# A memory-transformer block beside a mixer MLP: half of a weight loaded after the mixer's output stage, a fifth transpose buffer, segment sums and two constants later, one value product later in the tail

## The chip, the core and the metric

The kernel runs on one core of a Trainium2 chip. The metric is the device time in microseconds: the median of five runs, 1518.0 us before the change (1517.87 to 1518.15). A core has a matrix engine (TensorE, PE in the profile, with its weight loads shown apart as PEld), VectorE (DVE), ScalarE (ACT), GpSimd (POOL) and SyncE (SP, which here only issues DMA transfers). Each engine runs its own list of instructions in order; semaphores make one wait for another. Matmul results go to PSUM, a small memory from which DVE or ACT must take them before the buffer can be used again.

## What is computed

```python
xn = _layernorm(x)
return x + _A_ref(xn, ...) + _B_ref(xn, ...)

def _B_ref(x, w1, w2, w3, w4):                  # 2048 tokens, D = 1024, F = 3584
    h = _gelu(_layernorm(x) @ w1)
    ...                                         # four channel groups shifted by -1, +1, -2, +2 tokens
    x1 = x + hs                                 # hs = shifted h @ w2
    return x1 + _gelu(_layernorm(x1) @ w3) @ w4

def _A_ref(x, mem0, Wq, Wk, Wv, Wo, seg_len):   # 32 heads of 128, 8 memory rows, segments of 32 tokens
    for s in range(n_seg):
        h = concatenate([mem, xs])
        q, k, v = h @ Wq, h @ Wk, h @ Wv
        o = softmax(mask(q k^T * scale)) v @ Wo
        mem, out = o[:M], o[M:]
```

## The kernel before, in words

The program is written out by hand in the order in which each engine runs it. There are four stages, one after the other on PE.

**Start and w1 (lines 170 to 322).** x comes in 16 tiles of 128 tokens. For each tile DVE takes statistics (`ln_stats`, lines 199 to 207, the last step a power on POOL), writes a normalised copy (`ln_apply`, line 218; POOL makes the bias `nm` at line 220), and the copy is transposed. The first four tiles are transposed by PE (`pe_trans`, line 243, cast out of PSUM by DVE at 246 and ACT at 248), the others by a DMA transpose from SP's queue (`dma_trans`, line 223), behind which the next x tile and later w2 and w3 are queued. ACT overwrites x with its normalised form (`normalise_x`, line 235). Two tiles make a group; group g is multiplied by w1 in eight chains of eight matmuls (line 258 for groups 1 to 7, line 283 for group 0), and ACT takes each chain out of PSUM with a GELU (260, 288). The chains rotate through four PSUM buffers, "mm". Group 0 uses two larger buffers, "A" and "B", which the segment sums use after it: `seg_sums(n)` multiplies x tile n by the constant `segone`, 128x4, in eight small matmuls (line 253), and ACT copies the result to `xs` (254). Constants are loaded from POOL's queue by `const_tile` (line 106).

**Mixer output, w2 (lines 327 to 357).** For each of 16 tiles, two chains of eight matmuls (336); DVE adds x and takes statistics, POOL finishes them, ACT writes the normalised `xn3` (348, a ring of four buffers), POOL's queue stores x1 to a scratch tensor (349), and SP's queue transposes xn3 into `xn3T` (350). Behind each of the first eight transposes SP has one load of w3 (448 KB, `load_w3`, line 155). w3 has two halves of eight such pieces: w3a (0 to 7), w3b (8 to 15).

**MLP, w3 and w4 (lines 359 to 538).** SP's queue first loads the last four pieces of w3b, then w4 in seven loads of 1 MB, then what the residual needs (R and xt, 436 to 438). For each of four blocks of 512 tokens, PE runs 28 chains over w3 (514; chains 0 to 13 read w3a, 14 to 27 w3b), with a GELU by ACT (515), then w4 (532). `eye9` is used once at the start of this stage (372). Chunks of Wv and Wo are loaded in between (382, 384) into the place of an xn3T that PE has finished with.

**Attention (lines 545 to 913).** 32 steps (4 token blocks by 8 groups of 4 heads). In each step, PE projects q, k and v (579, 595, 602), and between these chains runs the score matmuls of the previous step's four sub-blocks (`scores`, 624, PSUM buffer "A") and the value products (`values`, 654, PSUM buffer "B"). DVE adds a term while it takes the product to `oX` (658), then ACT copies the memory columns to `oTm` (662), and the buffer is free. The output projection sums 32 heads (`out_part`, 751). After the last step s there is a hand-written tail (lines 880 to 912), in which scores and values of s alternate with output parts of 28 heads; p is the step before s. Its first lines are

```python
            scores(s, 0)
            values(p, 3)
            out_part(b, 0, 0, hp)
            scores(s, 1)
            values(s, 0)
            out_part(b, 1, 0, hp)
```

Of the kernel before, what the change touches and what calls it, by code (L numbers as in the profile page):

```python
# [13 lines left out]
BF16 = mybir.dt.bfloat16  # L14
# [7 lines left out]
P = 128  # L22
S = 2048
D = 1024
# [7 lines left out]
M = 8  # L32
# [31 lines left out]
def kernel(  # L64
# [37 lines left out]
    def const_tile(name, arr, dt=BF16, later=False):  # L102
        a = _bf(arr) if dt == BF16 else np.asarray(arr, np.float32)
        d = nc.inline_tensor(a, name=name)
        t = cpool.tile(list(arr.shape), dt, name=name + "_sb")
        load = lambda: nc.gpsimd.dma_start(t[:], d.ap())
        if later:
            return load, t
        load()
        return t  # L110

    tok = np.arange(P)
    segone_np = (tok[:, None] // SEG == np.arange(4)[None, :]).astype(np.float32)
# [5 lines left out]
    neghalf = cpool.tile([P, 2], F32)  # L119
    nc.gpsimd.memset(neghalf[:], -0.5)  # L120
    ident = const_tile("c_ident", np.eye(P, dtype=np.float32))
    segone = const_tile("c_segone", segone_np)
    eye9 = const_tile("c_eye9", np.concatenate([np.eye(M, dtype=np.float32), np.ones((M, 1), np.float32)], 1))
    load_qones, qones = const_tile("c_qones", np.repeat(segone_np[:, :, None], P, axis=2), later=True)
    load_causal, causal = const_tile("c_causal", causal_np, F32, later=True)
    load_mask40, mask40 = const_tile("c_mask40", _mask40(False), later=True)
# [36 lines left out]
    with ExitStack() as keepx:  # L163
# [6 lines left out]
        with ExitStack() as p0:  # L170
# [102 lines left out]
            pe_trans(1)  # L273
            normalise_x(0)
            normalise_x(1)
            first = []
            for tag in "AB":
                t = aux_tile([P, 2, 512], tag, "ps1")
# [14 lines left out]
            ln_stats(3)  # L293
            for n in (2, 3):
                ln_apply(n)
            for c0 in range(0, KT, 2):
                w1_first(c0, range(4, KT))
                w1_first(c0 + 1, range(4, KT))
                w1_first_out((c0, c0 + 1))
                if c0 in (2, 4):  # L300
                    pe_trans(c0 // 2 + 1)
            seg_sums(0)
            seg_sums(1)
            ln_stats(4)
            for g in range(1, NT // 2):
                nxt = [n for n in (2 * g + 2, 2 * g + 3) if n < NT]
                for n in nxt:
                    if n + 1 < NT:
                        ln_stats(n + 1)
                    ln_apply(n)  # L310
                    dma_trans(n)
                stage1(g, range(4))
                if g == 1:
                    normalise_x(2)
                    normalise_x(3)
                for n in nxt:
                    normalise_x(n)
                stage1(g, range(4, KT))
                seg_sums(2 * g)
                seg_sums(2 * g + 1)  # L320
# [6 lines left out]
        with ExitStack() as p2:  # L327
            ring = p2.enter_context(tc.tile_pool(name="p2ring", bufs=4))
            for n in range(NT):
                x1 = ring.tile([P, D], F32, tag="x1")  # L330
                st = ring.tile([P, 2, 6], F32, tag="st")
                for ch in range(2):
                    ps = mm_tile("ps2")
                    for k in range(KT):
                        o = 2 + n * P + SH[k]
                        nc.tensor.matmul(ps[:], hTB[:, k, o:o + P], w2_sb[:, k, ch * 512:(ch + 1) * 512], start=(k == 0), stop=(k == KT - 1))  # L336
                    nc.vector.tensor_tensor(x1[:, ch * 512:(ch + 1) * 512], ps[:], xts[n][:, ch * 512:(ch + 1) * 512], op=ALU.add)
                    nc.vector.bn_stats(st[:, ch, :], x1[:, ch * 512:(ch + 1) * 512])
                mv = ring.tile([P, 2], F32, tag="mv")
                nc.vector.bn_aggr(mv[:], st[:])  # L340
                a = ring.tile([P, 1], F32, tag="a")
                nc.gpsimd.tensor_scalar(a[:], mv[:, 1:2], EPS, None, op0=ALU.add)
                r3 = ring.tile([P, 1], F32, tag="r3")
                nc.gpsimd.tensor_tensor(r3[:], a[:], neghalf[:, 0:1], op=ALU.pow)
                nm3 = ring.tile([P, 1], F32, tag="nm3")
                nc.gpsimd.tensor_scalar(nm3[:], mv[:, 0:1], r3[:], -1.0, op0=ALU.mult, op1=ALU.mult)
                xn3 = ring.tile([P, D], BF16, tag="xn3")
                nc.scalar.activation(xn3[:], x1[:], ACTF.Identity, bias=nm3[:], scale=r3[:])
                nc.gpsimd.dma_start(R1_v[:, n, :], x1[:])
                nc.sync.dma_start_transpose(xn3Ts[n // 4][:, n % 4, :, :], xn3[:])  # L350
                if n < 8:
                    load_w3(4 + n)
                elif n == 8:
                    load_qones()
                    load_causal()
                    load_mask40()

    attx = main.enter_context(ExitStack())
    with ExitStack() as p3:
        big = p3.enter_context(tc.tile_pool(name="p3big", bufs=1))  # L360
        ring = p3.enter_context(tc.tile_pool(name="p3ring", bufs=3))
        for i in range(12, 16):
            load_w3(i)
        w4t = []
        for c in range(7):
# [448 lines left out]
    for i in range(NS):  # L814
        s = new_step(i)
        p = steps.get(i - 1)
        pp = steps.get(i - 2)
        fz = p is not None and p.b == 0
        last = i == NS - 1
        hooks = {}  # L820

        def at(c, f, *a):
            hooks.setdefault(c, []).append((f, a))

        if pp is not None:
            at(1, values, pp, 3)
        if p is not None:
            at(0, scores, p, 0)
            for m in range(3):
                at(3 * m + 3, scores, p, m + 1)  # L830
                at(3 * m + 4, values, p, m)
        if 4 < s.hg and s.b + 1 < NB:
            for k in range(3 * s.hg - 15, min(3 * s.hg - 12, KT)):
                at(2 + 4 * (k % 3), make_xm, s.b + 1, (k,))
        if fz:
            at(4, first_scores, p)
            at(8, first_soft, p)
            at(11, first_trans, p)
        if pp is not None and pp.b == 0:
            at(1, first_values, pp)  # L840
        if s.hg == 1 and s.b > 0:
            for c in range(8):
                at(1, out_chain, s.b - 1, c)
        if s.hg == 2 and s.b > 0:
            at(2, norm_sums, s.b - 1)
            for j in range(4):
                at((4, 5, 7, 8)[j], norm_recip, s.b - 1, j)
            at(10, norm_apply, s.b - 1)
            at(11, norm_add, s.b - 1)
        if s.hg == 0 and s.b > 0:  # L850
            load_Rt(s.b - 1, 0)
            load_Rt(s.b - 1, 1)
        for c in range(12):
            if c < 4:
                if c == 0 and s.b == 0:
                    mem_proj(s, "q", QM)
                q_chain(s, c)
                if c == 0:
                    mem_cols(s)
                if c == 3:  # L860
                    if i + 1 < NS:
                        need_w("k", i + 1)
                    if s.b == 0:
                        nc.sync.dma_start(wo_sb[:, hsl(s.hg), :], Wo_v[:, hsl(s.hg), :])
                    if s.hg == 4 and s.b + 1 < NB:
                        load_xT(s.b + 1)
            elif c < 8:
                k_chain(s, c - 4)
                if c == 7 and i + 1 < NS:
                    need_w("v", i + 1)  # L870
            else:
                v_chain(s, c - 8)
                if c == 11:
                    if s.b == 0:
                        mem_proj(s, "v", VM)
                    if i + 2 < NS:
                        need_w("q", i + 2)
            for f, a in hooks.get(c, ()):
                f(*a)
        if last:  # L880
            b = s.b
            load_Rt(b, 0)
            load_Rt(b, 1)
            hp = H - 4
            scores(s, 0)
            values(p, 3)
            out_part(b, 0, 0, hp)
            scores(s, 1)
            values(s, 0)
            out_part(b, 1, 0, hp)  # L890
            scores(s, 2)
            values(s, 1)
            out_part(b, 0, hp, H)
            out_part(b, 1, hp, H)
            out_part(b, 2, 0, hp)
            scores(s, 3)
            values(s, 2)
            out_part(b, 3, 0, hp)
            values(s, 3)
            out_part(b, 2, hp, H)  # L900
            out_part(b, 3, hp, H)
            norm_sums(b)
            for j in range(4):
                norm_recip(b, j)
            norm_apply(b)
            norm_add(b)
            out_chain(b, 4)
            out_chain(b, 5)
            verify()
            out_chain(b, 6)  # L910
            verdict()
            out_part(b, 7, 0, H, 2)
# [129 lines left out]
```

## Time and profile before

| | |
|---|---|
| median of 5 runs | 1518.0 us |
| the profiled execution | 1518.11 us |
| its span, first to last instruction | 1516.2 us |
| granted TensorE clock | 1.000 |
| busy: PE, DVE, ACT, POOL | 1497.0, 661.3, 453.1, 235.6 us |
| bytes moved by DMA | 208.38 MB, mean 137 GB/s |

A row of the order in time has the start and the duration in us, the engine, the line of the kernel, the operation, its output and inputs with their shape, how many instructions are merged in the row, and, in brackets, how long the engine was idle before it and what ended that. In PE's rows an instruction's end is modelled, so rows can overlap a little; starts are the better measure. SPq rows are DMA issues: they show when SP issued a transfer and for how long it was held up, not the transfer itself. A row that merges instructions can have gaps inside. The list of waits has who waited for whom, the total us, how many times, and the longest.

### The profile page before, as it was taken

What the parts mean: (1) busy time and instruction counts of PE and PEld (TensorE: products, weight loads), DVE (VectorE), ACT (ScalarE), POOL (GpSimd) and SP (SyncE); (2) the same over time, 40 slices, a digit from 0 to 9 for tenths busy, and PEclk for the clock granted to TensorE, in tenths of its full rate; (3) what the DMA queues carried; (4) which work ended last, traced back from release to release, by engine and by line L of the source; (5) the groups of instructions that cost most, each with busy time, mean ns of one, the idle gap of its engine ahead of it and who ended that gap; (6) DMA issues with size and microseconds to landing.
All of it is one profiled execution on the core that took longest, in us unless ns stands there. A gap on an engine that the chain in (4) does not pass through costs nothing.

```text
span 1516.2 us, 23927 instructions
## 1 busy us (share of the span) xinstructions
PE 1497.0 (99%) x9456; PEld 793.4 (52%) x9582; DVE 661.3 (44%) x1555; ACT 453.1 (30%) x1249; POOL 235.6 (16%) x652
## 2 busy tenths in 40 slices
PE   8999999999999999999999999999999999999998
PEld 6844444444444466666544444444544444444446
DVE  7284010010110226666622856731767640675652
ACT  5633202103012035454401344310433420344320
POOL 3142110111110211221200111110111110111100
PEclk9999999999999999999999999999999999999999
DMA  6699553553122545574522454421464431444211
GB/s 184 173 251 310 193 188 98 175 174 138 63 91 50 186 152 168 159 204 142 179 70 83 140 166 139 154 87 60 138 170 144 140 111 53 125 142 141 84 34 39
DMA packets 191029, 208.38 MB, mean 137 GB/s; under 512 B 51192, under 2 KB 158856, under 8 KB 190912
## 3 DMA queue, kind: packets, MB, share of 16 engines
q1 hardware_dynamic: 183664, 182.49, 39.9%
q0 software_dynamic: 7248, 24.31, 4.2%
q8 instruction: 77, 1.26, 0.3%
q14 instruction: 40, 0.33, 0.1%
HBM read 170.07 MB, written 25.17 MB: 129 GB/s over the span
## 4 chain that ended last, share of the span: by engine, by line
PE 97%; DVE 1%; ACT 1%; issue 1%; DMA 0%; DVEq 0%; ACTq 0%
PE psK L595 15%; PE psQ L579 15%; PE psP L751 15%; PE psV L602 14%; PE ps L514 13%; PE ps L532 13%; PE ps L336 4%; PE ps L258 3%; PE psO L654 2%; PE psS L624 2%; PE psM L611 1%; PE psY L773 1%; PE psvb L396 1%; PE psG L405 1%; PE ps L283 0%
## 5 line engine op out<-in xcount | busy, mean ns | idle before, releaser
L751 PE MATMUL psP<-wo_sb,oX 128*128 128x512 bf16 (+1 forms) x1036 | 221.5, 372 | 1.1
L628 ACT ACTIVATE ET<-psS 32x132 f32<-32x132 f32 x512 | 139.0, 272 | 195.3 <-PE psS L624 189.7
L532 PE MATMUL ps<-w,hT_all 128*128 128x512 bf16 x874 | 193.7, 379 | 1.2
L595 PE MATMUL psK<-xT,w 128*128 128x512 bf16 x747 | 176.3, 379 | 1.1
L579 PE MATMUL psQ<-xT,w 128*128 128x512 bf16 x750 | 175.9, 379 | 1.1
L602 PE MATMUL psV<-w,xT 128*128 128x512 bf16 x745 | 175.0, 379 | 1.0
L751 PEld LDWEIGHTS <-oX 128*128 128x128 bf16 x1056 | 102.8, 98 | 115.5
L595 PEld LDWEIGHTS <-w 128*128 128x128 bf16 x1280 | 121.3, 98 | 80.2
L579 PEld LDWEIGHTS <-w 128*128 128x128 bf16 x1024 | 96.8, 98 | 105.5 <-issue 1.3
L515 ACT ACTIVATE hT_all<-ps 128x512 bf16<-128x512 f32 x112 | 66.7, 597 | 283.9 <-PE ps L514 283.9
L532 PEld LDWEIGHTS <-hT_all 128*128 128x128 bf16 x896 | 87.2, 98 | 103.8
L662 ACT CAST oTm<-psO 128x16 bf16<-128x16 f32 x128 | 23.0, 179 | 357.1 <-DVE oX L658 357.1
L630 DVE STREAM_TRANSPOSE EQ<-ET 128x128 f32<-128x128 f32 x128 | 39.8, 311 | 172.3 <-ACT ET L628 172.0
L586 DVE TENSOR_TENSOR Q<-psQ,QM 128x512 bf16<-128x512 f32 (+1 forms) x128 | 85.3, 679 | 61.2 <-ACT Q L585 43.2
L645 POOL TENSOR_TENSOR BD<-ET,c_segone_sb 128x16 bf16<-128x16 f32 x128 | 33.9, 265 | 494.2 <-ACT ET L628 494.2
L602 PEld LDWEIGHTS <-xT 128*128 128x128 bf16 x768 | 72.1, 98 | 73.5
L514 PE MATMUL ps<-xn3T,w3a 128*128 128x512 bf16 x448 | 97.7, 379 | 0.0
L514 PE MATMUL ps<-xn3T,w3b 128*128 128x512 bf16 x448 | 97.7, 379 | 0.0
L643 DVE TENSOR_TENSOR BD<-PT,c_segone_sb 128x512 bf16<-128x512 bf16 x128 | 90.0, 703 | 4.4
L757 DVE TENSOR_TENSOR ot<-psP,Rt 128x512 bf16<-128x512 f32 (+1 forms) x33 | 22.2, 675 | 155.8 <-PE psP L751 155.8
L596 ACT CAST K<-psK 128x512 bf16<-128x512 f32 (+1 forms) x160 | 78.8, 506 | 33.6 <-PE psK L595 33.0
L440 DVE TENSOR_SCALAR xt<-xt,lnst 128x1024 bf16<-128x1024 bf16 x16 | 8.7, 546 | 181.7 <-POOL R L439 181.7
(157 smaller groups left out, 1619.4 us busy)
## 6 DMA issues: line engine op xcount, KB each, us to landing
w<-in_A_Wq_dram SPq DMA_DIRECT2D x32, 1024.0 KB, 5.7
w<-in_A_Wk_dram SPq DMA_DIRECT2D x32, 1024.0 KB, 5.7
w<-in_A_Wv_dram SPq DMA_DIRECT2D x32, 1024.0 KB, 5.7
R_scratch<-x POOLq DMA_DIRECT2D x16, 512.0 KB, 6.7
R<-R_scratch SPq DMA_DIRECT2D x16, 512.0 KB, 7.7
chunk<-in_A_Wv_dram SPq DMA_DIRECT2D x8, 1024.0 KB, 6.1
R_scratch<-R POOLq DMA_DIRECT2D x16, 512.0 KB, 6.4
chunk<-in_A_Wo_dram SPq DMA_DIRECT2D x8, 1024.0 KB, 6.4
```

The lines of the kernel that those rows point to most:

```text
L336: nc.tensor.matmul(ps[:], hTB[:, k, o:o + P], w2_sb[:, k, ch * 512:(ch + 1) * 512], start=(k == 0), stop=(k == KT - 1))
L514: nc.tensor.matmul(ps[:], w3[:, k, (f % FH) * P:(f % FH + 1) * P], xn3Ts[tb][:, :, k, :], start=(k == 0), stop=(k == KT - 1))
L515: nc.scalar.activation(h3T[:, f, :], ps[:], ACTF.Gelu_apprx_tanh)
L532: nc.tensor.matmul(ps[:], h3T[:, f, j * P:(j + 1) * P], w4t[f // 4][:, f % 4, ch * 512:(ch + 1) * 512], start=(f == 0), stop=(f == FT - 1))
L579: nc.tensor.matmul(ps[:], w[:, k, hh * P:(hh + 1) * P], s.xm[:, k, 0:512], start=(k == 0), stop=(k == KT - 1))
L586: nc.vector.tensor_tensor(q3[:, j0:16, 0:SEG], p3_[:, j0:16, :], QM[:, 4 * s.hg + hh, z + j0:z + 16].unsqueeze(2).to_broadcast((P, 16 - j0 ...
L595: nc.tensor.matmul(ps[:, 0:c], w[:, k, hh * P:(hh + 1) * P], s.xm[:, k, h2 * c:(h2 + 1) * c], start=(k == 0), stop=(k == KT - 1))
L596: nc.scalar.copy(s.K[:, hh, h2 * c:(h2 + 1) * c], ps[:, 0:c])
L602: nc.tensor.matmul(ps[:], s.xm[:, k, m * P:(m + 1) * P], w[:, k, :], start=(k == 0), stop=(k == KT - 1))
L628: nc.scalar.activation(ET[q, :, :], ps[q, :, W * j:W * (j + 1)], ACTF.Exp, scale=SCALE)
L643: nc.vector.tensor_tensor(B4[:, :, :, 0:SEG], PT[:].unsqueeze(2).to_broadcast((P, 4, 4, SEG)), so.unsqueeze(3).to_broadcast((P, 4, 4, SEG) ...
L751: nc.tensor.matmul(ps[:, 0:w], oX[:, h, m * P:(m + 1) * P], wo_sb[:, h, cc], start=(h == 0), stop=(h == H - 1))
```

## The change

Five edits. `segone` and `eye9` are no longer loaded at the top but on POOL's queue behind the first two tiles' normalisation. `ln_stats(4)` moves ahead of the second half of group 0, and the segment sums of tiles 0 and 1 from the end of group 0 to the middle of group 1, ahead of `normalise_x(2)` and `(3)`. The ring of `xn3` gets a fifth buffer. Only the first four transposes of the mixer's output stage are followed by a w3 load; all eight pieces of w3b are loaded at the start of the MLP stage, ahead of w4. In the tail, `values(p, 3)` comes after the first output part instead of before it. No matmul is added or removed.

```diff
-    segone = const_tile("c_segone", segone_np)
-    eye9 = const_tile("c_eye9", np.concatenate([np.eye(M, dtype=np.float32), np.ones((M, 1), np.float32)], 1))
+    load_segone, segone = const_tile("c_segone", segone_np, later=True)
+    load_eye9, eye9 = const_tile("c_eye9", np.concatenate([np.eye(M, dtype=np.float32), np.ones((M, 1), np.float32)], 1), later=True)
...
             normalise_x(0)
             normalise_x(1)
+            load_segone()
+            load_eye9()
...
             for n in (2, 3):
                 ln_apply(n)
+            ln_stats(4)
             for c0 in range(0, KT, 2):
...
                 if c0 in (2, 4):
                     pe_trans(c0 // 2 + 1)
-            seg_sums(0)
-            seg_sums(1)
-            ln_stats(4)
...
                 stage1(g, range(4))
                 if g == 1:
+                    seg_sums(0)
+                    seg_sums(1)
                     normalise_x(2)
                     normalise_x(3)
...
-                xn3 = ring.tile([P, D], BF16, tag="xn3")
+                xn3 = ring.tile([P, D], BF16, tag="xn3", bufs=5)
...
-                if n < 8:
+                if n < 4:
                     load_w3(4 + n)
...
-        for i in range(12, 16):
+        for i in range(8, 16):
             load_w3(i)
...
             scores(s, 0)
+            out_part(b, 0, 0, hp)
             values(p, 3)
-            out_part(b, 0, 0, hp)
             scores(s, 1)
```

## The prediction

> **What bounds the kernel now.** I read the page's head and its first two parts, then the chain of waits, then TensorE's own waits, and last the order in time at the three places that the change touches.
>
> ```profile
> span 1516.2 us, 23927 instructions
> ...
> PE 1497.0 (99%) x9456; PEld 793.4 (52%) x9582; DVE 661.3 (44%) x1555; ACT 453.1 (30%) x1249; POOL 235.6 (16%) x652
> ...
> PEclk9999999999999999999999999999999999999999
> ...
> PE 97%; DVE 1%; ACT 1%; issue 1%; DMA 0%; DVEq 0%; ACTq 0%
> ```
>
> TensorE (PE) is busy for 1497.0 of 1516.2 us, at full granted clock, and is 97% of the chain that ended last. The change adds and removes no matmul. So it can only give back part of the 1516.2 - 1497.0 = 19.2 us in which PE is idle, or add to them. PE's waits say where those lie:
>
> ```profile
> PE ps L258 <- ACT hT_all L260: 1.4, 1, 1.4
> ...
> PE psO L654 <- ACT oTm L662: 1.0, 1, 1.0
> PE psX L253 <- ACT hT_all L288: 0.6, 1, 0.6
> ```
>
> The columns are total us, times, longest. These three, 3.0 us in all, stand where the change works. The rest is elsewhere: the table by stretches has 4.6 us of idle in the first 20 us and 3.8 in the last 16, and about 0.05 per 10.8 us between. PE's order in time around the first two waits:
>
> ```profile
> 20.09 0.34 PE L253 MATMUL psX<-c_segone_sb,x 128*128 128x4 bf16 x8
> 20.99 0.34 PE L253 MATMUL psX<-c_segone_sb,x 128*128 128x4 bf16 x8 [0.57 <-ACT hT_all L288]
> 21.20 7.15 PE L258 MATMUL ps<-xn2T,w_sb 128*128 128x256 bf16 x64
> 28.18 0.54 PE L253 MATMUL psX<-c_segone_sb,x 128*128 128x4 bf16 x16
> 30.11 7.15 PE L258 MATMUL ps<-xn2T,w_sb 128*128 128x256 bf16 x64 [1.39 <-ACT hT_all L260]
> ```
>
> ScalarE (ACT) in the same stretch:
>
> ```profile
> 24.89 0.38 ACT L260 ACTIVATE hT_all<-ps 128x256 bf16<-128x256 f32 x1 [0.49 <-PE ps L258]
> 25.17 4.62 ACT L235 ACTIVATE x<-x,nm,lnst 128x1024 bf16<-128x1024 bf16 x4
> 29.69 1.18 ACT L260 ACTIVATE hT_all<-ps 128x256 bf16<-128x256 f32 x4
> ```
>
> The four normalisations hold ACT for 4.5 us, PE fills its four PSUM buffers meanwhile, and waits until the first GELU after them.
>
> **Segment sums, one group later.** Before, the sums of tile 1 wait for ACT to empty the accumulator that they reuse, so group 1 starts at 21.20. Now w1's group 1 comes straight after the last first-group matmuls. Its PSUM buffers must be emptied by the transposes' casts, and ln_stats(4) now stands before those on VectorE (DVE): the stats take 21.21 - 19.34 = 1.87 us and would run 16.12 to 17.99, so tile 2's cast moves from 17.41 to 17.99. Tile 3's cast still waits for PE at 18.73 and ends at 19.42. Both are done before 20.1: no cost, with 0.7 us of cover; without it, what is late is PE itself. x of tile 4 is there: DMA engines fall idle near 15 us and its statistics show no DMA wait. Group 1 then starts at about 20.1, 1.1 us earlier.
>
> That isn't kept in full. Four chains later (GELU 3 was at 21.20 + 3.69) GELU 3 ends at about 24.2 instead of 25.27. Now the 16 small matmuls follow (0.40 us of PE) and ACT has two xs copies (0.28 for the pair in the later row) ahead of the normalisations. The second copy needs its sums, at 20.11 + 3.53 + 0.54 = 24.18, and ends at about 24.4. So the normalisations start at about 24.35 instead of 25.17, and PE's restart at 30.11 moves by the same 0.8 us, to 29.3. PE itself arrives at 28.0 (28.72 before) and still waits about 1.3 us: the wait stays nearly whole, ACT's chain decides. **Gain 0.8 us.** From below: 0.3, if copies and normalisations don't overlap. From above: 1.1, the whole shift of the group's start. The inputs of group 2 come sooner too: DVE's chain for tiles 4 and 5 loses the 1.87 us that the stats stood behind, so the transpose of tile 5 goes to SyncE's queue (SP) at 24.1 instead of 25.98. With the landing times of this tile, 3.2 to 5.2 us, it is there by 29.3 at the worst.
>
> **Two constants later on GpSimd (POOL).** Their issues, 0.557 and 0.538 us, leave 1.99 to 3.07, where POOL next waits 2.56 us for DVE: nothing is gained there. They go behind the nm pair that ends at 9.02, and end at about 10.1; POOL's next operation is at 12.75. The data, 7.2 us from issue to landing, are there by 16.8; segone is first read at 23.6, eye9 at 129.8. One doubt: DVE's normalisation of tile 1 starts at 9.07 for 0.54 us, and PE's transposes wait for it. Rows first: the POOL power op takes 0.70 us alone (12.75) and 0.92 beside such a DVE op (14.61), while thirteen of these DVE ops keep to 535 to 545 ns whatever POOL does. The Trainium skill, "SBUF — State Buffer", section "Who interferes with whom", states that a DVE op in a two-port mode and a GpSimd op exclude each other for a whole instruction, and that the first to issue wins. By the rows POOL loses and PE pays nothing. By the rule, POOL would issue 0.05 us earlier, win, and cost PE up to 0.56 us in the start-up. No run here shows a POOL DMA issue beside this DVE op; I take the rows, 0, and keep 0.56 for the range.
>
> **Half of w3 behind the mixer's output stage, and a fifth xn3 buffer.** In that stage PE is busy 4.95 to 5.00 of every 5 us, so quicker transposes (ACT waited 3.8 us once for a buffer) give PE nothing: 0. What moves are four loads of 448 KB on SP, to the end of the transposes. SP's order there:
>
> ```profile
> 137.16 2.19 SPq L155 DMA_DIRECT2D w3b<-in_B_w_dram  x4
> 139.85 12.37 SPq L367 DMA_DIRECT2D w<-in_B_w_dram  x7
> 152.27 2.58 SPq L436 DMA_DIRECT2D R<-R_scratch  x1
> 154.90 0.56 SPq L438 DMA_DIRECT2D xt<-in_A_x_dram  x1
> 178.61 0.38 SPq L382 DMA_DIRECT2D chunk<-in_A_Wv_dram  x1
> ```
>
> PE first reads w3b at 154.24, now at 153.4. The last xn3 is ready at 134.47 - 0.8, and the transposes have less ahead of them, so the eight loads begin at about 136. Eight loads are 3.67 MB; at the 370 to 390 GB/s that the table shows from 140 on, 10 us plus landing put the last at 147 to 148: 5 us of cover. Behind them stand w4 (first read at 178.4; the DMA engines fell idle at 165, now by about 169), the first R and xt (0.5 and 0.25 MB, consumed by POOL at 167, now 171; DVE adds into R only after 184), and then SP waits 23.1 us for PE before the next load. All of the 4.75 us (1.84 MB at 387 GB/s) is swallowed by that. **Cost 0.** If the cover fails, PE stalls at f = 14 for whatever is missing.
>
> **Tail.** PE now, with the wait:
>
> ```profile
> 1444.21 0.39 PE L624 MATMUL psS<-Q,K 128*128 128x132 bf16 x4
> 1445.64 0.41 PE L654 MATMUL psO<-BD,V 128*128 128x132 bf16 x4 [1.04 <-ACT oTm L662]
> 1445.89 6.20 PE L751 MATMUL psP<-wo_sb,oX 128*128 128x512 bf16 x28
> 1451.93 0.39 PE L624 MATMUL psS<-Q,K 128*128 128x132 bf16 x4
> 1452.16 0.40 PE L654 MATMUL psO<-BD,V 128*128 128x132 bf16 x4
> ```
>
> values(p, 3) waits for the one psO buffer. After the change the 28 heads start at 1444.21 + 0.24 = 1444.45 (their buffer was emptied at about 1441; they read token block 0 of oX, values(p, 3) writes block 3), and values(p, 3) follows 6.04 us later, at 1450.49, without a wait. But values(s, 0) wants the same psO only two steps later. How long a psO is held, an undisturbed case tells: matmuls at 1473.17, DVE's oX 1473.61 to 1474.30, ACT's oTm 1474.34 to 1474.52, and 0.06 to PE: 1.41 us. So values(s, 0) can start at 1451.90, not at 1450.96: a new wait of about 0.95 us takes the place of the one removed. Against 1452.16 before, **gain 0.26 us**. Bounds: 0, if the new wait is as long as the old (1.2 by start times), and 1.2, if it is hidden. Behind the waiting matmuls stands the whole of out_part 1; scores(s, 1) has its exponentials after oTm on ACT, which 6 us of out_part cover.
>
> **Sum.** 0.8 + 0 + 0 + 0.26 = 1.06 us. The profiled execution took 1518.11 us (span 1516.2 and 1.9 around it), 0.11 above the median; a span of 1515.1 gives 1517.05 in its terms, and against the median of 1518.0, 1516.95. I say 1517.0. A measurement can tell about 0.2%, 3.0 us: by size this is no change.
>
> **Rivals.**
> - The waits only move (chance 0.20): ACT gives back only 0.3 us at group 2, the tail's new wait equals the old, and POOL's issues cost part of 0.56: 1518.0 - 0.3 + 0.2 = 1517.9. For it speaks that both places have a second wait just behind the first; against it, the computed starts.
> - More than I count (0.10): the whole 1.1 at group 1 and a hidden psO, 1518.0 - 2.1 = 1515.9. It needs ACT's chain not to bind, against the row at 25.17.
> - w3b comes late (0.08), the slower side. Between 136 and 153.4 the queue must bring 3.67 MB, beside about 1 MB of R1 writes still going out: 4.7 MB in 17.4 us is 270 GB/s, and below that PE stalls at f = 14. Between 120 and 140 the table shows 184, 274, 353 and 268 GB/s, with transposes among the loads, so it isn't out of reach. At 200 GB/s it takes 23.5 us, 6.1 too late: 1517.0 + 6.1 = 1523.1. Against it: the loads come after the transposes, and from 140 on the rate was never below 370 while loads were queued.
> - My forecast, 0.6. The last 0.02 are left for faster by over 3 us: there isn't that much idle time at these places, so only an effect that I don't see could give it.
>
> Faster by over 0.2% 0.02, within 0.2% 0.90, slower by over 0.2% 0.08. The range 1515.8 to 1518.2 takes in the first two rivals and leaves out the third.
>
> **What would show it.** Group 1's first w1 matmul near 20.1 and group 2's near 29.3, with a wait of about 1.3 us for ACT there; DVE's second normalisation still at 9.07; no PE wait at the first w3b matmul near 153.4; in the tail no wait at the first psO and one of about 0.8 us, in that list's way of counting, at the next. I am wrong if PE waits for a DMA anywhere between 130 and 190, or if a PE wait shows elsewhere that was not there before.

## The result and the profile after

The changed kernel takes 1516.76 us (median of 42 runs, 1516.42 to 1517.67), the kernel before 1518.16 (79 runs beside them, 1517.54 to 1532.09). The ratio of the means is 0.9979, with a 95% interval of 0.9970 to 0.9987: faster by 0.21%, not the 0.07% that I forecast. The medians alone differ by 1.40 us, close to my 1.06. The rest is in the spread, which the five times that I had did not show: of the 79 runs of the kernel before, 22 took more than 1519 us; of the 42 after, none. Without those 22, the median before is 1518.08. So there are two effects: 1.32 us in the typical execution, and about 1.9 us in the mean (1520.03 - 1516.80 - 1.32) from executions that are now and then 1 to 14 us longer and that the change took away. Below I call a run long when it is over 1519 us.

The profiled execution after took 1516.79 us. The page's head, PE's waits and PE's order in time around the first two waits:

```profile
span 1514.9 us, 23923 instructions
...
PE 1497.5 (99%) x9456; PEld 793.5 (52%) x9582; DVE 661.5 (44%) x1555; ACT 452.4 (30%) x1249; POOL 235.3 (16%) x652
```

```profile
PE ps L258 <- ACT hT_all L260: 1.2, 1, 1.2
...
PE psO L656 <- ACT oTm L664: 0.8, 1, 0.8
```

```profile
20.05 3.66 PE L258 MATMUL ps<-xn2T,w_sb 128*128 128x256 bf16 x32
23.54 0.54 PE L253 MATMUL psX<-c_segone_sb,x 128*128 128x4 bf16 x16
23.95 3.65 PE L258 MATMUL ps<-xn2T,w_sb 128*128 128x256 bf16 x32
27.44 0.54 PE L253 MATMUL psX<-c_segone_sb,x 128*128 128x4 bf16 x16
29.17 7.15 PE L258 MATMUL ps<-xn2T,w_sb 128*128 128x256 bf16 x64 [1.19 <-ACT hT_all L260]
```

Group 1 starts at 20.05 instead of 21.20, group 2 at 29.17 instead of 30.11: 0.94 us, of which 0.04 came before the edits' place. ACT's normalisations start at 24.21 (24.35 expected). In the tail:

```profile
1443.22 0.39 PE L626 MATMUL psS<-Q,K 128*128 128x132 bf16 x4
1443.45 6.21 PE L753 MATMUL psP<-wo_sb,oX 128*128 128x512 bf16 x28
1449.50 0.40 PE L656 MATMUL psO<-BD,V 128*128 128x132 bf16 x4
1449.73 0.39 PE L626 MATMUL psS<-Q,K 128*128 128x132 bf16 x4
1450.89 0.41 PE L656 MATMUL psO<-BD,V 128*128 128x132 bf16 x4 [0.76 <-ACT oTm L664]
```

From the first scores to the second values product it is now 7.67 us, where it was 1452.16 - 1444.21 = 7.95: a gain of 0.28, with the new wait where it was expected. PE reads w3b from 153.30 on without a wait. All of this is as forecast, and none of it explains the 22 long executions of the kernel before.

What the two profiles do show on that is in the mixer's output stage. In these two, a transpose of xn3 took 3.1 to 12.8 us to land before (median 5.8), and 3.1 to 6.8 after (median 4.4). In the table by stretches, the last two columns are the busy share of the DMA engines and the GB/s that they moved. The share adds up the time that packets took, so overlapping packets bring it above 1. Before, then after:

```profile
120.00:125.00 5.00, 5.00 (x25) 2.29 (x24) 4.10 (x8) 1.25 (x2) 1.83 (x5) 1.00 1.15 184
125.00:130.00 5.00, 4.95 (x30) 2.21 (x29) 4.31 (x8) 1.98 (x3) 2.87 (x8) 1.00 1.20 274
```

```profile
120.00:125.00 5.00, 5.00 (x25) 2.25 (x23) 4.34 (x8) 1.24 (x1) 2.59 (x7) 1.00 0.87 244
125.00:130.00 5.00, 4.95 (x31) 2.25 (x30) 4.25 (x8) 2.48 (x2) 2.34 (x6) 1.00 0.74 203
```

In the profile before, the DMA engines are saturated until the stage ends; in the one after, they have caught up. ACT's last normalisation of the stage and its first GELU of the MLP, before:

```profile
124.18 1.24 ACT L348 ACTIVATE xn<-x,nm,r 128x1024 bf16<-128x1024 f32 x1 [3.75 <-DMA xn3T<-xn]
...
133.23 1.24 ACT L348 ACTIVATE xn<-x,nm,r 128x1024 bf16<-128x1024 f32 x1 [2.31 <-POOL nm L346]
134.38 1.66 ACT L515 ACTIVATE hT_all<-ps 128x512 bf16<-128x512 f32 x3
```

PE starts the MLP at 130.06, and its four PSUM buffers hold four chains of 1.73 us, until 136.97. The first GELU empties one at 134.98: 2.0 us of cover. The GELU stands on ACT behind the last xn3, and an xn3 can't be written before an old transpose has left its buffer. That gave my theory, A: when the transposes land a few us later than in this profile, ACT stands still, and PE with it. The rivals were B, that the edits of group 1 or of the tail took the long executions away, and C, chance or the chip.

### The profile page after: what moved, and what is told of

The parts are those of the page before. It is cut to its first block, busy times and chain, and to the rows that moved or that the text cites. A ratio compares the mean times of both kernels' runs of the same rounds, so it can differ in the third digit from the quotient of the medians.

```text
span 1514.9 us, 23923 instructions
## 1 busy us (share of the span) xinstructions
PE 1497.5 (99%) x9456; PEld 793.5 (52%) x9582; DVE 661.5 (44%) x1555; ACT 452.4 (30%) x1249; POOL 235.3 (16%) x652
## 4 chain that ended last, share of the span: by engine, by line
PE 95%; DVE 2%; ACT 1%; issue 1%; DMA 0%; DVEq 0%; ACTq 0%
PE psP L753 15%; PE psQ L581 14%; PE psK L597 14%; PE psV L604 14%; PE ps L516 13%; PE ps L534 13%; PE ps L338 4%; PE ps L258 3%; PE psO L656 2%; PE psS L626 2%; PE psM L613 1%; PE psY L775 1%; PE psvb L398 1%; PE psG L407 1%; PE ps L285 0%
```

## The experiments

### Which edit takes the long executions away

All four ran on one chip beside 67 runs of the kernel before, of which 19 were long.

Mixer stage undone in the changed kernel:

```diff
-                xn3 = ring.tile([P, D], BF16, tag="xn3", bufs=5)
+                xn3 = ring.tile([P, D], BF16, tag="xn3")
...
-                if n < 4:
+                if n < 8:
...
-        for i in range(8, 16):
+        for i in range(12, 16):
```

> The changed kernel with the mixer's output stage as before (four xn3 buffers, eight w3 loads behind its transposes). The typical execution: 1516.8 us, like the changed kernel, since that stage's edits gave PE nothing in the two profiles. Theory A (that stage's transfers now and then hold up PE, and the change took that away): about a quarter of the executions come out 2 to 14 us longer again, as 20 of 79 did before. Rival B (the group 1 or tail edits took it away): no execution over 1518. Rival C (chance, or the chip): long executions on some chips with every kernel.

Measured: 3 of 14 long, median 1516.95; without the long ones 1516.86. The long executions are back. The other one of the pair is the reverse, the kernel before with these three lines changed and nothing else:

> The kernel before with only the mixer stage's edits (fifth buffer, half of w3 later). Typical execution 1518.0 us by both theories. Theory A: no long executions, none over 1519. Rival B: about a quarter are 2 to 14 us longer, as before.

Measured: none of 22 long, 1517.70 to 1518.38, median 1517.89, ratio 0.9988 (0.9977 to 0.9999). B falls: this stage's edits alone do it, and with them the typical execution changes little (1517.89 against 1518.02, the median of the kernel before without its long runs). C is unlikely: all ran on one chip, and with 19 of 67 long, a kernel that is no different would show none in 22 about once in 1500 times. Then each half of the edit, the first with only the second and third of the hunks above:

> The changed kernel with all eight w3 loads back behind the mixer's transposes, the fifth xn3 buffer kept. Typical 1516.8 us. Theory A in the form that the loads' traffic delays transposes and x1 stores: long executions come back (a tenth to a quarter). In the form that the missing fifth buffer is the cause: none. Rival B: none.

Measured: 5 of 22 long (up to 1534.46), median 1516.88. And with only the first hunk:

> The changed kernel with four xn3 buffers instead of five, the w3 loads late. Typical 1516.8 us. Theory A in the form that the loads' traffic is the cause: no long executions. In the form that the fifth buffer is what helps: a tenth to a quarter long. Rival B: none.

Measured: 1 of 22 long (1529.02), median 1516.78. Where the loads stand is what counts: with them back, 5 of 22 are long, as before; with them late, one, and that few would come by chance in under 1% of cases if the kernel were like the one before. One in 22 is too few to say whether the fifth buffer takes away a rest.

### Where the time goes in a long execution

The changed kernel, with four buffers and all of w3 in the stage:

```diff
-                xn3 = ring.tile([P, D], BF16, tag="xn3", bufs=5)
+                xn3 = ring.tile([P, D], BF16, tag="xn3")
...
-                if n < 4:
+                if n < 12:
                     load_w3(4 + n)
-                elif n == 8:
+                if n == 8:
...
-        for i in range(8, 16):
-            load_w3(i)
```

> The changed kernel with four xn3 buffers and all twelve remaining w3 pieces behind the mixer stage's first twelve transposes, none after: four more loads in that stage than before. Theory A (the loads' traffic delays that stage's transposes and stores until PE runs out of PSUM buffers): at least as many long executions as the 3 of 14 and 5 of 22 with eight loads, likely a third or more, and longer ones; in the profile transposes that take over 10 us to land, waits of ACT for xn3T and of DVE for the x1 stores, of several us. Typical execution 1516.8 to 1519. Rival (what counts is only where w3b's first pieces stand, not the traffic): no more long ones than with eight loads.

Measured: 11 of 14 long, beside 16 of 51 for the kernel before, median 1526.87, up to 1540.08, and the profiled execution is a long one (1529.86). Its waits, and ACT's and PE's order in time where the stage ends:

```profile
ACT xn L350 <- DMA xn3T<-xn: 22.6, 4, 8.0
...
PE ps L514 <- ACT hT_all L515: 11.4, 1, 11.4
```

```profile
136.50 1.24 ACT L350 ACTIVATE xn<-x,nm,r 128x1024 bf16<-128x1024 f32 x1 [5.37 <-DMA xn3T<-xn]
145.73 1.24 ACT L350 ACTIVATE xn<-x,nm,r 128x1024 bf16<-128x1024 f32 x1 [7.99 <-DMA xn3T<-xn]
146.88 2.04 ACT L515 ACTIVATE hT_all<-ps 128x512 bf16<-128x512 f32 x4
```

```profile
129.02 7.08 PE L514 MATMUL ps<-xn3T,w3a 128*128 128x512 bf16 x32
147.51 18.79 PE L514 MATMUL ps<-xn3T,w3a 128*128 128x512 bf16 x80 [11.41 <-ACT hT_all L515]
```

PE runs through the mixer stage without a break, makes four chains of the MLP (32 matmuls), and then waits 11.4 us. The GELUs are next on ACT, but the normalisations of the last tiles stand ahead of them, the very last waiting 8 us for a transpose. No one needs these tiles before the MLP's last block.

The kernel before once more, and the two other edits by themselves:

> The kernel before once more, for its profile. By the counts so far (41 of 146 over 1519 us) one such look is long with a chance of about 0.28; Theory A expects then a PE wait in the mixer stage or at its end, behind late transposes or stores. Otherwise 1518.0 us and a profile like the first.

It was not a long one: 1518.2 us, transposes landing after at most 9.0 us. The second profile of it went the same way, 1518.2 us and at most 10.7:

> The kernel before, for a profile of a long execution (about one in three of its executions on these chips). Theory A: if long, the PE stall lies at the MLP's fifth chain, for ACT behind late transposes. If short, a profile like the first.

So a long execution of the kernel before itself was never profiled; that its stall is at the same place is inferred from its variants. Its recorded clocks fit that. Of the 195 runs of the kernel before beside these experiments, the 38 with a mean granted clock of 0.998 or less are all long, by over 4 us. The three long executions that were profiled (this one with twelve loads and two below) had 0.997, 0.997 and 0.994, and there it is PE's standstill that lowers the clock. Where PE stands still the mean can't tell.

> The kernel before with only the edits of the first stage: constants later, statistics and segment sums moved. My sum for it was 0.8 us, the profile after shows the second group's start 0.94 us earlier (0.04 of it before the edits' place): typical execution 1517.1 us. Long executions as often as before, since the mixer stage is unchanged.

Measured: 1517.39 us without its 5 long runs of 20, against 1518.22 for the kernel before beside it: 0.83 us.

> The kernel before with only values(p, 3) behind the first output part. My sum for it was 0.26 us, the profile after shows 0.27: typical execution 1517.8 us. Long executions as often as before.

Measured: 1517.88 without its 7 long runs of 20: 0.34 us. The two make 1.17 of the 1.32 us, the mixer stage's edits alone another 0.13, and neither of the two has fewer long executions. The ratios over all runs, 0.9998 (0.9976 to 1.0019) and 0.9995 (0.9975 to 1.0016), can't tell such amounts from nothing while long runs are mixed in.

If ACT's queue is what carries the delay to PE, the transposes may stay late as long as nothing on ACT waits for them. The kernel with twelve loads, but the last three tiles' xn3 made by DVE at the stage's end (cut to the new loop; ACT's normalisation and the transpose of these tiles are left out above it):

```diff
...
+            for n, x1, r3, nm3 in held:
+                xn3 = ring.tile([P, D], BF16, tag="xn3")
+                nc.vector.tensor_scalar(xn3[:], x1[:], r3[:], nm3[:], op0=ALU.mult, op1=ALU.add)
+                nc.sync.dma_start_transpose(xn3Ts[n // 4][:, n % 4, :, :], xn3[:])
```

> The kernel with all twelve pieces in the mixer stage (11 of 14 executions long, median 1526.9 us), but the last three tiles' xn3 made by DVE behind that stage's other DVE work, so that ACT has no operation that waits for a transpose ahead of the first GELUs. The transposes stay as late. Theory A in its last form (PE stalls because ACT's queue stands behind those transposes): no stall at the first chains of the MLP, typical execution 1516.8 to 1517.5 us, long ones under a fifth. Rival (PE stalls for the late transfers themselves, w3b or x1): still mostly long, median over 1522.

Measured: 1 of 22 long (1520.0), median 1517.16. Its transposes still take up to 13.6 us to land (median 7.4), and DVE waits 3.4 us for one. On ACT the first GELU waits for PE's first chain only:

```profile
130.86 0.60 ACT L524 ACTIVATE hT_all<-ps 128x512 bf16<-128x512 f32 x1 [8.12 <-PE ps L523]
```

With the rows of the long execution above, that shows the carrier: late transposes cost PE time where ACT's queue stands behind them. The profile is of a short execution, and the edit also issues the last transposes a little later, so how late they are in its slowest executions is not known.

### What makes the transposes late

The kernel before, with its eight loads put two behind each of the first four transposes:

```diff
-                if n < 8:
-                    load_w3(4 + n)
+                if n < 4:
+                    load_w3(4 + 2 * n)
+                    load_w3(5 + 2 * n)
```

> The kernel before with the same eight loads in the mixer stage, but two behind each of the first four transposes instead of one behind each of the first eight. Theory A (the backlog at the stage's end counts: transposes late there hold ACT's last normalisations, with the first GELUs of the MLP queued behind them): the backlog has the second half of the stage to drain, so long executions are rarer than with the kernel before, under a tenth. Rival (the traffic as such, anywhere in the stage, counts): as often as before, a quarter. Typical execution 1518.1 us.

Measured: 11 of 22 long (25 of 52 of the kernel before beside it), median 1519.21. My expectation fell: earlier loads do not help. Its profile, of a short execution, offers a reason: the DMA engines' share is 1.03 or more in every stretch from 90 to 130, which leaves no slack for a backlog to drain. That made the question whether the sum of the transfers counts, or the loads in SP's queue. The kernel before, half of the x1 stores left out:

```diff
-                nc.gpsimd.dma_start(R1_v[:, n, :], x1[:])
+                if n < 8:
+                    nc.gpsimd.dma_start(R1_v[:, n, :], x1[:])
...
-            nc.sync.dma_start(R1[:], R1_v[:, n, :])
+            nc.sync.dma_start(R1[:], R1_v[:, n % 8, :])
```

> The kernel before with its eight w3 loads in the mixer stage, but x1 stored only for the first eight of sixteen tiles (4 MB less written in that stage's second half; the second half of the residual is read from the first half's rows, so the output is not the reference's there). Theory A, with the DMA engines' total work in the stage as what counts: no long executions, since more is taken away than the four loads of the change (1.8 MB); the DMA engines' share falls well below 1 before 130. Rival (the loads themselves, on SP's queue among the transposes, are what delays them): a quarter or more long, as with the kernel before. Typical execution 1518.1 us.

Measured: none of 21 long, 1517.76 to 1518.26, beside 8 of 25 for the kernel before. The loads are all in place, on the same queue; other transfers, from POOL's queue, are gone, and so are the long executions. The DMA engines' share falls far below 1:

```profile
120.00:125.00 5.00, 5.00 (x25) 2.27 (x24) 4.33 (x9) 1.49 (x2) 1.34 (x5) 1.00 0.28 55
```

So it takes more than the loads among the transposes: taking away loads or stores is enough. That is what the stage's total work for the DMA engines as the cause would do. Whether a byte of stores counts like a byte of loads was not tested; the stores left out are 4 MB, the loads that the change moves 1.8.

Two more profiles of the kernel with early loads, for its long executions:

> The kernel with the eight loads behind the first four transposes, for a profile of one of its long executions (11 of 22 were over 1519 us). Theory A, total work: if long, PE stalls some 7 us after the MLP's first matmul, for GELUs that stand behind ACT's last normalisations, as in the kernel with twelve loads; transposes land after 10 us and more. Rival: a stall elsewhere, at w3b's first chain or within the mixer stage.

> The same once more, since a look is long only every second time: if long, Theory A expects the PE stall within the first four chains of the MLP, the rival elsewhere.

Both were long, 1531.12 and 1537.92 us. PE's row after the first four chains, in the first and in the second:

```profile
148.25 19.04 PE L515 MATMUL ps<-xn3T,w3a 128*128 128x512 bf16 x80 [11.24 <-ACT hT_all L516]
```

```profile
154.31 20.11 PE L515 MATMUL ps<-xn3T,w3a 128*128 128x512 bf16 x80 [16.30 <-ACT hT_all L516]
```

The same place, and ACT's waits for xn3T are 24.9 and 29.8 us in all. Transposes land after up to 16.8 and 18.2 us. In the second, PE also waited 0.76 us for DVE before its third chain. With PE's slower clock after the stall (last section), the waits make 12.9 and 19.7 us, of the 13.0 and 19.8 by which these executions exceed the kernel's short median of 1518.14: nothing else is left to explain.

The second profile also shows that bytes are not the whole of the work. Its last load in the stage was issued by 101.6 us, and still the transposes stayed late for 50 us more. From 130 to 145, with only transposes and x1 stores, the DMA engines moved 180 GB/s at a share of 1.18; in the short execution of the same kernel they moved 280 at 1.15 from 105 to 130. In a long execution the same transfers keep the engines busy for longer. What starts that is not shown.

### A version with the two remaining waits taken away

```diff
-                for n in nxt:
-                    normalise_x(n)
+                if g > 1:
+                    for n in nxt:
+                        normalise_x(n)
                 stage1(g, range(4, KT))
+                if g == 1:
+                    for n in nxt:
+                        normalise_x(n)
...
             values(p, 3)
+            out_part(b, 1, 0, 4)
             scores(s, 1)
             values(s, 0)
-            out_part(b, 1, 0, hp)
+            out_part(b, 1, 4, hp)
```

> The changed kernel with its two remaining waits taken away: in group 1 the normalisations of tiles 4 and 5 come behind the second half's chains (so ACT's GELUs 4 to 7 stand ahead of them), and in the tail four heads of output part 1 stand between values(p, 3) and scores(s, 1), so that psO has 0.9 us more to be emptied. Expected from the profile after: minus 1.2 at group 2, minus 0.7 in the tail: typical execution 1514.9 us. Long executions none, as with the changed kernel, since the mixer stage is the same.

Measured: 1514.65 us, ratio to the kernel before 0.9961 (0.9942 to 0.998), and 2.1 us under the changed kernel's median, where I expected 1.9. Group 2 starts without a wait at 27.99, and neither wait for psO nor that for group 2 is left in PE's list. One of its 15 runs was long (1524.52): with the change's mixer stage, long runs are 1 of 79 over three kernels (0 of 42, 0 of 22, 1 of 15), against 90 of 274 for the kernel before. Rare is not never: in the profile of this version, a short execution, a transpose took up to 12.5 us to land and the DMA engines' share was 1.09 and 1.10 from 120 to 130, much as in the kernel before. The slack in the one profile after is not in every execution.

## Why the prediction was right and wrong

**Right, by its own steps.** Segment sums: 0.8 us forecast, 0.90 in the profile (0.94 less the 0.04 that came earlier), 0.83 for that edit alone. Tail: 0.26 forecast, 0.28 in the profile, 0.34 alone, and the wait that takes the other's place was 0.76 us at the place named. Constants: no cost; DVE's normalisation of tile 1 still takes 0.54 us and starts 0.61 us after the cast ahead of it, as before. w3b: the eight loads were issued from 134.90 to 139.1 and no wait followed. The typical execution came out 0.24 us below the 1517.0 forecast. Two small sums were off and bear on nothing: PE's idle time between 240 and 1460 us is 8.0 us, 0.07 per 10.8 and not 0.05; and the rival that gains more would by its own bounds, 1.1 and 1.2, come to 1515.7.

**Wrong: the step on the mixer stage.** It says that "quicker transposes (ACT waited 3.8 us once for a buffer) give PE nothing: 0". That holds in the profiled execution, and I took one execution for all. The five times that I had were bad luck here: with a third of the executions long, five short ones in a row come about once in eight times. The step counted PE's idle time inside the stage, where there is none in a long execution either; it named no work that covers ACT's wait, and no place where the cover ends. The cover could be read: 2.0 us behind the stage's last normalisation, with one transpose at 12.8 us and DMA engines that had more than full work at the very end. Priced as a risk, this was a gain: a third of the executions by some 1 to 17 us. In the changed kernel's comparison it is worth 1.9 us in the mean, more than the two edits that I did price. The 0.02 that I left for an effect that I didn't see was this term.

The same view was used for the rival on the slower side. I looked for a late transfer that the change might make, and not for one that it might remove.

**Open.** Why the transposes are slow in one execution and not in the next was not found; the runs show only that it is frequent where the stage is saturated and goes when its transfers are fewer. The fifth buffer's own part was not settled.

## What to carry to other kernels

One profile shows one execution. Where a stage keeps the DMA engines at a share near or above 1, find the instruction that waits for its last transfer, what stands behind that on the same engine, and how many us of cover there are: an operation that nobody needs soon can hold up one that everybody needs. Here, moving such transfers within the saturated stretch gained nothing; moving them out of it did, and so did taking the waiting operation off the engine that PE depends on.

## What the runs showed of the hardware

With transposes and the end of an x1 store left to do, the DMA engines can be fully busy and move little. In the second long execution of the kernel with early loads, at two stretches where PE stands still (granted clock, DMA share and GB/s are the last three columns):

```profile
145.00:150.00 5.00, 0.00 (x0) 0.00 (x0) 0.00 (x0) 0.77 (x1) 0.00 (x0) 0.50 1.33 81
150.00:155.00 5.00, 0.69 (x2) 0.25 (x2) 0.00 (x0) 2.94 (x5) 0.00 (x0) 0.50 1.11 164
```

A share of 1.33 with 81 GB/s, where plain loads of w4 in the profile after moved 387 to 409 at 1.03 to 1.05. Transposes one at a time, in the run without half of the stores, took less: 1.05 MB at a share of 0.365 over the 15 us from 120, where the transposes above moved 0.98 MB at 1.147 over 10 us, over twice the engine time per byte.

The stall also costs PE its clock: the granted clock was 1.00 until PE stood still and 0.50 when it started again. In the first of the two long executions the 80 matmuls up to w3b took 167.13 - 148.25 = 18.9 us, where 80 at the full rate (12.08 us for 56, later in the same profile) take 17.3.

A POOL DMA issue that started 0.11 us ahead of DVE's normalisation (8.92 against 9.03) took 0.77 us instead of 0.56, while the DVE operation kept its 0.54. That is the doubt of the prediction: by the rule that it cites, DVE would have had to wait for the issue, and in this one row it did not.
